# A planned attention-and-mixer kernel on one core: row sums, split loads, an uneven last chunk and small-tile products in one change

## The chip, the cores and the metric

One Trainium2 chip, one of its NeuronCores. TensorE (PE) does the matrix products, VectorE (DVE), ScalarE (ACT) and GpSimd (POOL) the rest, SyncE (SP) issues nearly all transfers. The metric is the device time of one execution in microseconds (us); less is better. Three timed runs of the kernel before gave 359.39, 359.53 and 359.98 us.

## The reference, cut to what matters

Linear attention over 8 batches of 8 heads, 576 tokens and 64 dimensions, then a mixer block on the 512 joined columns. All inputs and the output are float32.

```python
kv = einsum('bhsd,bhse->bhde', k, v)          # 64 x 64 for each head
out = einsum('bhsd,bhde->bhse', q, kv)
x = out / sqrt(mean(out * out, -1) + 1e-6) * g_norm      # heads joined: [8, 576, 512]
a1 = alpha1 * x + beta1
u = x + lam * einsum('ts,bsd->btd', w_tok, a1)           # w_tok: 576 x 576
a2 = alpha2 * u + beta2
result = u + lam * (maximum(a2 @ w_ch1, 0) @ w_ch2)      # 512 -> 2048 -> 512
```

The term `beta1` of `a1` goes through the token weight as (row sum of `w_tok`) times `beta1`. So the kernel carries one extra row beside the transposed token weight: the 576 row sums.

## The kernel before, in words

**Stages.** For each batch: the product k.v for 64 x 64 blocks (L691 for batch 0 and batches 2 to 7, L794 and L804 for batch 1), the product q.kv (L924 and L947 for batch 0 in float32; L1012, L454 and L1095 later), the norm, the token mixing (L1238 for batch 0, then L1161, L1213, L1192), the first channel layer (L1339, L1351, L1324 for even batches, L1366 for odd ones) with a relu on ACT, and the second channel layer (L1415; L1396 for the last 128 tokens). The 576 tokens of a batch are four chunks of 128 and a tail of 64; the tails of two batches are joined into a fifth chunk of the odd batch.

**The start.** Batch 0 needs everything at once: SP loads k, v and q of batch 0 by halves of four heads, then the token weight (L1516 and L1519, staged in the buffer `ht`), then batch 1 and the channel weights. q.kv of batch 0 (L915) multiplies 64-row by 128-column pieces of the transposed q by 64 columns of kv. The token weight is transposed by TensorE in five groups (L1556, `wt_groups`, L1546) and a tail group (L1570); ACT and DVE copy each to `wt` in bf16. Its row sums were made by TensorE: ten products of `wt` with a selecting matrix `sel` (L1592), whose result row is copied to row 64 of the fifth piece of `wt`. The product of that piece (the `rtt,wt` rows of L1238) needs the row.

**The order of the work** is made by a planner in the kernel's own text. Every operation is recorded with an engine, a cost, and what it reads and writes (L73). `plan` (L125) ranks operations by the time to the marked ones (`due`, L1656) and lays them out with `schedule` (L177), eight times over; a table of numbers then moves single operations (L1732). `schedule` books each load with a length (`dma_us`) and 1.75 us to completion (L348). It also books TensorE's instructions in blocks of 256 and lets no operation start whose block has not come by its table (L209). Until the first marked operation (the first channel layer of batch 0) is placed, TensorE is given a small product on zeros (L1728, called a filler here) wherever the plan has nothing ready for it. Fillers are real instructions: they take their time on the chip whether or not the wait exists there. `synchronize` (L370) then puts in the waits.

**The end.** The last 128 tokens of the last batch (`halves`, L1389) are done as two pieces of 256 output columns: 16 products, an addition on DVE (L1402) and a store (L1405) each.

## Time and profile before

| what | value |
|---|---|
| timed runs, median | 359.53 us |
| the profiled execution's own time | 358.89 us |
| its span, first to last instruction | 357.0 us |
| TensorE busy | 348.2 us (98%) |
| VectorE, ScalarE, GpSimd busy | 235.9, 157.1, 24.5 us |
| granted TensorE clock | 1.000 |

The profile is of one execution. A row of the chain of waits has a start, a length and what ran; a row of a timeline adds the shapes and, in brackets, idle time of the engine ahead of the row and what ended it. A group's row has the busy time, the mean of one instruction in ns, and the idle time before. Matrix products overlap in the array, so a single one's length (379 ns for 512 columns) is more than its share of the engine; the step from one start to the next is the price.

### The profile page before, as it was taken

How to read it: one execution, taken by the hardware profiler on the slowest of the kernel's cores; microseconds unless marked ns; L12 is line 12 of the kernel's file. 1: busy time of each engine (PE TensorE's matmuls, PEld its weight loads, DVE VectorE, ACT ScalarE, POOL GpSimd, SP SyncE). 2: the span in 40 equal slices, each digit the busy share in tenths (PEclk: the TensorE clock that was granted, in tenths of full speed). 3: DMA queues.
4: the chain of work that ended last, by engine and by line, in shares of the span. 5: the costliest groups of instructions: out<-in, count | busy, mean ns of one | idle time of the engine just before them, and what ended most of it. 6: DMA issues, size and time to landing. Idle time of an engine off the chain costs nothing.

```text
span 357.0 us, 7694 instructions
## 1 busy us (share of the span) xinstructions
PE 348.2 (98%) x3460; PEld 203.9 (57%) x3278; DVE 235.9 (66%) x359; ACT 157.1 (44%) x274; POOL 24.5 (7%) x31
## 2 busy tenths in 40 slices
PE   8999999999999999999999999999999999999996
PEld 6777554487645544467644554457644554457644
DVE  3577899778982489947884389957984378830021
ACT  3454981258810494028810386018830285007500
POOL 4153032700000000000000000000000000000000
PEclk9999999999999999999999999999999999999999
DMA  8999999789457830599257870395145010150022
GB/s 282 355 344 360 404 342 369 277 142 277 160 132 210 274 137 3 118 196 326 103 118 152 243 271 0 73 207 166 30 113 153 31 31 0 31 160 3 0 59 88
DMA packets 79896, 60.15 MB, mean 169 GB/s; under 512 B 53037, under 2 KB 63541, under 8 KB 79736
## 3 DMA queue, kind: packets, MB, share of 16 engines
q1 hardware_dynamic: 79840, 59.67, 56.5%
q8 instruction: 26, 0.43, 0.5%
q14 instruction: 6, 0.05, 0.0%
q10 hardware_dynamic: 24, 0.01, 0.0%
HBM read 38.82 MB, written 9.44 MB: 135 GB/s over the span
## 4 chain that ended last, share of the span: by engine, by line
PE 94%; DVE 2%; issue 1%; DMA 1%; ACT 0%; SPq 0%
PE ps L1415 31%; PE ps L1366 20%; PE ps L1324 14%; PE ps L1161 7%; PE ps L691 5%; PE ps L1012 2%; PE ps L454 2%; PE ps L1192 1%; PE ps L1238 1%; DMA vf<-in_v_dram 1%; PE ps L1273 1%; PE ps L924 1%; PE ps L1396 1%; PE ps L1213 1%; PE ps L1095 1%
## 5 line engine op out<-in xcount | busy, mean ns | idle before, releaser
L1415 PE MATMUL ps<-w,ht 128*128 128x512 bf16 x538 | 122.1, 379 | 2.1 <-issue 1.4
L1415 PEld LDWEIGHTS ps<-w,ht 128*128 128x128 bf16 x560 | 53.6, 98 | 63.7 <-issue 2.0
L1313 ACT ACTIVATE ht<-ps,hb 128x512 bf16<-128x512 f32 (+1 forms) x96 | 70.9, 739 | 43.2 <-PE ps L1366 31.8
L1366 PE MATMUL ps<-a2t,w 128*128 128x320 bf16 (+1 forms) x512 | 72.4, 299 | 0.0
L1366 PEld LDWEIGHTS ps<-a2t,w 128*128 128x128 bf16 x512 | 49.4, 98 | 20.2
L1324 PE MATMUL ps<-a2t,w 128*128 128x512 bf16 x231 | 53.3, 379 | 0.8 <-issue 0.5
L762 ACT ACTIVATE kvd<-ps 64x128 bf16<-64x128 f32 x24 | 6.5, 272 | 94.5 <-PE ps L691 94.3
L1425 DVE TENSOR_TENSOR xm<-ps,xm 128x512 f32<-128x512 f32 x31 | 20.7, 688 | 29.7 <-PE ps L1415 29.6
L1324 PEld LDWEIGHTS ps<-a2t,w 128*128 128x128 bf16 x240 | 22.6, 98 | 25.7
L1161 PE MATMUL ps<-rt,wt 128*128 128x512 bf16 x106 | 24.8, 379 | 0.3
L1034 DVE TENSOR_REDUCE small<-sq 128x16 f32<-128x1024 f32 x14 | 16.9, 1214 | 9.1 <-ACT sq L1032 9.0
L1314 ACT ACTIVATE ht<-ps 128x512 bf16<-128x512 f32 (+1 forms) x32 | 20.2, 655 | 3.0 <-PE ps L1324 1.8
L1174 DVE TENSOR_TENSOR xm<-ps,xm 128x1024 f32<-128x1024 f32 x14 | 17.1, 1222 | 5.1 <-PE ps L1213 4.0
L767 DVE TENSOR_TENSOR kvd<-ps,kvd 64x128 bf16<-64x128 f32 x24 | 6.9, 289 | 20.3 <-ACT kvd L762 19.9
L691 PEld LDWEIGHTS ps<-vf,kf 64*64 64x64 f32 x1008 | 16.0, 135 | 5.9 <-issue 4.8
L691 PE MATMUL ps<-vf,kf 64*64 64x64 f32 x1008 | 17.9, 221 | 0.5 <-DMA vf<-in_v_dram 0.5
L1161 PEld LDWEIGHTS ps<-rt,wt 128*128 128x128 bf16 x112 | 10.9, 98 | 12.9 <-issue 0.4
L646 DVE TENSOR_TENSOR qs<-qf,qs 128x1024 bf16<-128x1024 f32 x14 | 16.9, 1218 | 0.8 <-ACT qs L560 0.7
L1053 DVE TENSOR_TENSOR xm<-ps,small 128x1024 f32<-128x1024 f32 x14 | 17.1, 1224 | 0.4
L1425 DVE TENSOR_TENSOR xtl<-ps,xtl 128x512 f32<-128x512 f32 x4 | 2.8, 692 | 21.1 <-PE ps L1415 21.0
L1180 DVE TENSOR_TENSOR a2b<-xm,a_bc 128x512 bf16<-128x512 f32 x24 | 15.5, 688 | 0.4
L1012 PEld LDWEIGHTS ps<-kvd,qt 128*128 128x128 bf16 x224 | 14.1, 98 | 2.4
(148 smaller groups left out, 349.2 us busy)
## 6 DMA issues: line engine op xcount, KB each, us to landing
out_dram<-xm SPq DMA_DIRECT2D x31, 256.0 KB, 2.7
qf<-in_q_dram SPq DMA_DIRECT2D x7, 1024.0 KB, 7.7
kf<-in_k_dram SPq DMA_DIRECT2D x6, 1152.0 KB
vf<-in_v_dram SPq DMA_DIRECT2D x6, 1152.0 KB, 9.6
stg<-in_moe_w_ch_dram SPq DMA_DIRECT2D x3, 1024.0 KB, 13.7
kf<-in_moe_w_ch_dram SPq DMA_DIRECT2D x2, 1024.0 KB
kf<-in_k_dram SPq DMA_DIRECT2D x2, 576.0 KB, 4.7
vf<-in_v_dram SPq DMA_DIRECT2D x2, 576.0 KB, 6.2
```

Source lines behind the costliest of these rows:

```text
L646: lambda e, hi=hi, lo=lo, src=src: e.tensor_tensor(out=lo, in0=src, in1=hi, op=ALU.subtract), r=kin + kh, w=kl, port=True)
L691: m = e.matmul(t.ap(slice(64 * x, 64 * x + 64))[:, y, 0:64], nine(kf, b, a)[r, x, c, :], nine(vf, b, a)[r, x, c, :], start=(c == 0), stop= ...
L1012: e.matmul(o, w, kvd[:, h, 0, :], start=True, stop=False)
L1053: P.op("DVE", dve_us(64 * m), lambda e: e.tensor_tensor(out=x3, in0=split(raw()), in1=inv, op=ALU.mult), r=[t, ("sm", sms)], w=xk, pri=-200)
L1161: m = e.matmul(t.ap()[:, i, :], tok_w(sc, c), rsrc(b, sc), start=(sc == 0), stop=(sc == 4))
L1174: P.op("DVE", dve_us(512 * n), lambda e: e.tensor_tensor(out=x, in0=t.ap(rows) if n > 1 else t.flat(rows), in1=x, op=ALU.add), r=[t] + xk, ...
L1313: o = P.op("ACT", act_us(n) + 0.07 * (b > 1), lambda e: e.activation(dst, src(), ACT.Relu, bias=hb[:, fj:fj + 1]) if b > 1 else e.activati ...
L1314: dst, src(), ACT.Relu, bias=hb[:, fj:fj + 1]) if b > 1 else e.activation(
L1324: m = e.matmul(t.flat(), w, a2t[:, dj, 0:512], start=(dj == 0), stop=(dj == 3))
L1366: m = e.matmul(t.ap()[:, i, 0:n], w1[:, dj, 128 * fj:128 * fj + 128], a2t[:, dj, 320 * i:320 * i + n], start=(dj == 0), stop=(dj == 3))
L1415: m = e.matmul(t.flat(), ht[:, fj, 128 * c:128 * c + 128], w2[:, fj, :], start=(fj == 0), stop=(fj == 15))
L1425: P.op("DVE", dve_us(512), lambda e: e.tensor_tensor(out=x, in0=t.flat(), in1=x, op=ALU.add), r=[t] + keys, w=keys)
```

## The change

**Row sums from the loaded rows.** The selecting matrix and the ten products at L1592 go. Instead each of the five pieces of the loaded token weight (four of 128 rows, one of 64, each 576 columns wide) is summed along its columns by ACT or DVE into one column of a new tile `rs`, and five float32 products with the identity turn these columns into one row, which is copied to `wt`. **Two loads.** The token weight's first 512 rows come in two loads instead of one, and the transposes are grouped by load: six groups of four or two transposes instead of five groups of four. **q.kv in quarters.** For batch 0 each product of 128 columns becomes two of 64: twice the products, each in a quarter of the array. **The last chunk** is split into 384 and 128 columns. **The plan** gets other lengths for several transfers, a time to completion for each of the transposing transfers, more marked operations (all of the first layer of batch 1, the second layer of batch 1, the first operation of batch 2) and a new table of 42 moves.

```diff
-    def op(self, eng, cost, fn, r=(), w=(), pri=0.0, dma_us=None, port=False, ins=8):
+    def op(self, eng, cost, fn, r=(), w=(), pri=0.0, dma_us=None, port=False, ins=8, after=1.75):
...
-                        pick.end = dma_free + 1.75
+                        pick.end = dma_free + pick.after
...
-        sel = sb("sel", [128, 128], BF16)
+        rs = sb("rs", [128, 5], F32)
...
-                        w=[("qt", c, 0), ("qt", c, 1)], dma_us=2.0)
+                        w=[("qt", c, 0), ("qt", c, 1)], dma_us=1.3, after=0.9)
...
-                            for x in range(2):
-                                kr = slice(64 * x, 64 * x + 64)
-                                o = 256 * c + 64 * h
-                                mm = e.matmul(ts[x].flat()[:, o:o + 64], qt32[kr, 4 * a + h, c, :],
-                                              kv32[kr, a, (h + 2 * x) % 4, :], start=True,
-                                              stop=True, skip_group_check=True)
+                            for sh in range(2):
+                                for x in range(2):
+                                    kr = slice(64 * x, 64 * x + 64)
+                                    o = 256 * c + 64 * h
+                                    mm = e.matmul(
+                                        ts[x].flat(slice(64 * sh, 64 * sh + 64))[:, o:o + 64],
+                                        qt32[kr, 4 * a + h, c, 64 * sh:64 * sh + 64],
+                                        kv32[kr, a, (h + 2 * x) % 4, :], start=True, stop=True,
+                                        skip_group_check=True)
...
-                    r=[("a2b", c)], w=[("a2t", c)], pri=-200, dma_us=1.0)
+                    r=[("a2b", c)], w=[("a2t", c)], pri=-200, dma_us=0.8, after=1.0)
...
-                for i in range(2):
-                    t, cols = P.ptile(1), slice(256 * i, 256 * i + 256)
+                for lo, n in ((0, 384), (384, 128)):
+                    t, cols = P.ptile(1), slice(lo, lo + n)
...
-        P.op("SP", 0.6, lambda e: e.dma_start(
-            wst, moe_w_tok[0:512, :].rearrange("(p c) s -> p c s", c=4)),
-            w=["wst"], dma_us=3.3)
+        for i in range(2):
+            P.op("SP", 0.6, lambda e, i=i: e.dma_start(
+                wst[:, 2 * i:2 * i + 2, :],
+                moe_w_tok[0:512, :].rearrange("(p c) s -> p c s", c=4)[:, 2 * i:2 * i + 2]),
+                w=[("wst", i)], dma_us=1.6)
...
+            def total(i):
+                dst = rs[:, i:i + 1] if i < 4 else rs[0:64, 4:5]
+                src = wst[:, i, :] if i < 4 else wst2
+                junk = w1[:, i, 0:576] if i < 4 else w1[0:64, 0, 576:1152]
+                key = ("wst", i // 2) if i < 4 else "wst2"
...
+                    if e is nc.scalar:
+                        return e.activation(junk, src, ACT.Identity, accum_out=dst)
+                    return e.tensor_reduce(out=dst, in_=src, axis=AX.X, op=ALU.add)
...
-                    for sc in range(5):
-                        n = 128 if sc < 4 else 64
-                        m = e.matmul(t.flat()[:, 0:hi - lo], sel[0:n, :], wt[0:n, sc, lo:hi],
-                                     start=(sc == 0), stop=(sc == 4))
+                    for tc in range(5):
+                        n = 128 if tc < 4 else 64
+                        i = OFF[tc] if tc < 4 else 4
+                        m = e.matmul(t.flat()[:, 128 * tc:128 * tc + n],
+                                     rs[0:n, i:i + 1].to_broadcast([n, 128]), ident[0:n, 0:n],
+                                     start=True, stop=True, skip_group_check=True)
...
-            elif (b, ch, i) == (1, 0, 0):
-                due[o] = 36
+            elif (b, ch) == (1, 0) and i == int(i):
+                due[o] = 36 + 1.1 * i
+            elif (b, ch) == (1, 1):
+                due[o] = 56 + 0.87 * i
+            elif (b, ch, i) == (2, 0, 0):
+                due[o] = 78
```

How TensorE's instructions stand, at three places. The lines of the changed kernel are a few numbers further on: L1728 became L1772 (fillers), L924 L927, L947 L952, L691 L693, L1556 L1564, L1570 L1587, L1238 L1243, L1592 gave way to L1633, L794 L796. A float32 product that stands once here is two instructions in the trace.

First place, TensorE from the two small products that end the parameters (L1471, now L1476) to the transposes of the token weight. Before:

```order
L1728 MATMUL ps<-a2b 128x512 x2
L924 MATMUL ps<-kvd,qt 128x64 x16
L691 MATMUL ps<-vf,kf 64x64 x16
L947 MATMUL ps<-kvd,qt 64x64 x4
L1728 MATMUL ps<-a2b 128x512 x3
L691 MATMUL ps<-vf,kf 64x64 x20
L726 MATMUL ps<-ident,qf 128x128 x8
L1728 MATMUL ps<-a2b 128x512 x4
L741 MATMUL ps<-ident,qft 128x64 x2
L924 MATMUL ps<-kvd,qt 128x64 x16
L947 MATMUL ps<-kvd,qt 64x64 x4
L1728 MATMUL ps<-a2b 128x512
```

and of the change:

```order
L1772 MATMUL ps<-a2b 128x512 x3
L952 MATMUL ps<-kvd,qt 64x64 x4
L1772 MATMUL ps<-a2b 128x512
L927 MATMUL ps<-kvd,qt 64x64 x32
L1772 MATMUL ps<-a2b 128x512 x3
L693 MATMUL ps<-vf,kf 64x64 x36
L728 MATMUL ps<-ident,qf 128x128 x8
L743 MATMUL ps<-ident,qft 128x64 x2
L1772 MATMUL ps<-a2b 128x512 x3
L1564 MATMUL ps<-ident,ht 128x128 x8
L952 MATMUL ps<-kvd,qt 64x64 x4
L1564 MATMUL ps<-ident,ht 64x128 x2
```

The second k.v product is no longer cut in two; transposes of the token weight now stand ahead of the second half of q.kv (which follows these rows as 32 products of L927), and ten fillers have stayed ten.

Second place, TensorE around the token mixing of batch 0. Before:

```order
L1728 MATMUL ps<-a2b 128x512
L1238 MATMUL ps<-rt,wt 128x256 x12
L1592 MATMUL ps<-wt,sel 128x512 x5
L1592 MATMUL ps<-wt,sel 128x64 x5
L1238 MATMUL ps<-rt,wt 128x256 x4
L1728 MATMUL ps<-a2b 128x512 x2
L1238 MATMUL ps<-rtt,wt 128x256 x4
```

and of the change:

```order
L1772 MATMUL ps<-a2b 128x512 x7
L1243 MATMUL ps<-rt,wt 128x256 x16
L1633 MATMUL ps<-ident,rs 128x128 x4
L1633 MATMUL ps<-ident,rs 128x64
L1772 MATMUL ps<-a2b 128x512
L796 MATMUL ps<-vf,kf 64x64 x16
L1243 MATMUL ps<-rtt,wt 128x256 x4
```

Seven fillers stand where one stood, one where two stood, the ten sums are five products, and the first k.v product of batch 1 has moved up ahead of the mixing's last piece.

Third place, TensorE from the token mixing of batch 2 to its first channel layer. Before:

```order
L1161 MATMUL ps<-rt,wt 128x512 x16
L1213 MATMUL ps<-rtt,wt 128x512 x4
L1415 MATMUL ps<-w,ht 128x512 x60
L691 MATMUL ps<-vf,kf 64x64 x36
L1415 MATMUL ps<-w,ht 128x512 x8
L691 MATMUL ps<-vf,kf 64x64 x36
L1415 MATMUL ps<-w,ht 128x512 x4
L1324 MATMUL ps<-a2t,w 128x512 x8
```

and of the change, from the products of the second layer of batch 1 that now stand ahead of the mixing:

```order
L1420 MATMUL ps<-w,ht 128x512 x24
L1100 MATMUL ps<-kvd,qt 64x64 x16
L1420 MATMUL ps<-w,ht 128x512 x16
L1166 MATMUL ps<-rt,wt 128x512 x16
L1420 MATMUL ps<-w,ht 128x512 x4
L1218 MATMUL ps<-rtt,wt 128x512 x4
L1420 MATMUL ps<-w,ht 128x512 x36
L693 MATMUL ps<-vf,kf 64x64 x72
L1329 MATMUL ps<-a2t,w 128x512 x12
```

Of the second layer of batch 1, 72 products stood between the mixing of batch 2 and its first layer; now 36 do, and 40 of them stand between the second main piece of q.kv of batch 2 and the mixing, where 72 products of the first layer (L1366) and 8 of the second stood.

More of the change, by code (lines that the diff above doesn't have):

```diff
@@ L24 @@
     __slots__ = ("eng", "cost", "fn", "deps", "alloc", "tiles", "pri", "idx",
-                 "start", "end", "pos", "waits", "inc", "lat", "ring", "clock", "port", "follow", "ins")
+                 "start", "end", "pos", "waits", "inc", "lat", "after", "ring", "clock", "port", "follow", "ins")
     def __init__(self, eng, cost, fn, pri, idx):
@@ L1603, in run @@
+            yield row
         def run(gens):
```

102 lines of the change are left out of this document (61 added, 41 removed), and 9 rows, old and new, of the table start.

## The prediction

> **What bounds the kernel now.** I read the busy time by stretch first. The first row below is the start, up to the first channel layer of batch 0; the second runs from there to the last product; the third is the end. Columns: length, then busy time (and instructions) of PE, its weight loads, DVE, ACT, POOL, then granted clock, DMA share, GB/s.
>
> ```profile
> 5.99:34.05 28.06, 27.48 (x430) 22.14 (x436) 19.56 (x41) 13.50 (x33) 9.61 (x12) 1.00 1.05 353
> 34.05:353.70 319.65, 316.43 (x2986) 177.94 (x2798) 214.70 (x314) 142.07 (x240) 11.08 (x7) 1.00 0.53 152
> 353.70:357.00 3.30, 0.03 (x1) 0.00 (x0) 0.43 (x1) 0.00 (x0) 0.00 (x0) 1.00 0.12 41
> ```
>
> PE is busy for 316.43 of 319.65 us in the middle. Its list of waits says what the rest is:
>
> ```profile
> PE ps L1415 <- issue: 1.4, 9, 0.2
> PE ps L691 <- DMA vf<-in_v_dram: 0.5, 1, 0.5
> PE ps L1324 <- issue: 0.5, 3, 0.2
> ```
>
> Twelve gaps of about 0.16 us, each "issue", that is, for nothing another engine does. So the middle cannot become shorter by a better order; it can only become longer by new waits. What the change can win lies in the 28.06 us of the start and the 3.30 us of the end. For the start I use the chain of waits, whose steps are PE's own (start, length, what):
>
> ```profile
> 7.27 1.05 PE ps L1495 x2
> ...
> 10.52 1.93 PE ps L924 x32
> 12.45 0.62 PE ps L691 x32
> ...
> 13.47 0.59 PE ps L1728 x2
> 14.06 0.74 PE ps L691 x40
> ...
> 16.96 1.79 PE ps L924 x31
> 18.75 0.38 PE ps L947 x8
> ...
> 22.73 1.47 PE ps L1238 x12
> 24.20 1.54 PE ps L1592 x10
> 26.28 0.43 PE ps L1728 x2
> ...
> 33.50 0.39 PE ps L804 x16
> ```
>
> Even here PE never idles longer than 0.16 us, because the plan has put fillers (L1728) where it foresaw waits. The price of the start is therefore the sum of PE's instructions, fillers included.
>
> **The start, term by term.** All terms lie on PE, which sets the end.
>
> Sums removed: the ten products at L1592, -1.54.
>
> Row added: five float32 products, ten instructions, eight of 128 columns and two of 64, 1152 columns in all. The nearest row is L1495, float32 with 512 columns: two instructions, 1024 columns, 1.05 us. So 1152 / 1024 x 1.05 = +1.18. Were only one pass needed it would be 0.59; that is the lower bound.
>
> Quarters: now 1.93 + 0.06 + 1.79 = 3.78 us for 64 instructions, 59 ns each. The nearest row for the new shape is the k.v product of a later batch, same 64 x 64 pieces, same 64 columns, same cycling through four quarters:
>
> ```profile
> 114.93 1.21 PE ps L691 x72
> ```
>
> 16.8 ns each; 128 instructions cost 2.15. The upper bound is L804, also in quarters but short: 0.39 us for 16, 24.4 ns, so 3.12. I take the first, since the new runs are 64 long: -1.63 (bounds -1.63 and -0.66). The Trainium skill, "TensorEngine Tiling (Array Packing)", section "Instruction Overhead", says that each matmul has about 60 cycles of overhead, so that one should not tile a dimension that is already small; with the 2.4 GHz of the Trainium skill, "Trainium Kernel Development and Optimization", section "NeuronCore Architecture", that is an estimated 25 ns a piece, 3.2 us, and would leave of the start's sum below about nothing. L691's 16.8 speaks against it, L804's 24.4 for it.
>
> Fillers: after the first k.v product there were 13, now 18 (the order rows: ten stay ten, three become eight). Two cost 0.43, so five cost +1.08. The second k.v product in one piece, 1.21 for 0.62 + 0.74: -0.15.
>
> Sum of the start: -1.54 + 1.18 - 1.63 + 1.08 - 0.15 = -1.06. The first layer starts near 33.0 instead of 34.05.
>
> **What must hide.** The row sums go to DVE (three) and ACT (two). A DVE reduction of 512 columns is half of the first row here; the others are two loads, with their issue (start, length) and, from the list of transfers, KB and us to landing:
>
> ```profile
> 13.13 1.28 DVE L897 TENSOR_REDUCE small<-sq 128x8 f32<-128x512 f32 x2 [2.84 <-ACT sq L895]
> 6.74 0.59 SPq L1516 DMA_DIRECT2D ht<-in_moe_w_tok_dram x1
> ht<-in_moe_w_tok_dram SPq DMA_DIRECT2D x1, 1152.0 KB, 10.0
> 14.89 1.65 SPq L604 DMA_DIRECT2D vf<-in_v_dram  x1
> vf<-in_v_dram SPq DMA_DIRECT2D x1, 1024.0 KB, 8.9
> ```
>
> With 576 columns about 0.7 each, 2.1 us more on DVE between 15 and 20 us. Cover: the seven fillers (1.5 us) ahead of the mixing, which stood at 22.73 and comes to 22.73 - 1.63 - 0.15 + 6 x 0.216 = 22.25. By my count q.kv's second half ends near 19.6; two squares and two reductions, each step about 0.6, bring DVE to 21.6, and a copy of the token weight to 22.1. Without the fillers 1.4 us of that would show. The first reduction waits for the first load; queued behind it on DVE are a reciprocal and the second multiplication (L905) of the first half, which POOL and then the mixing wait for. The old load landed at 6.74 + 10.0 = 16.7; half of it, 576 KB at 353 GB/s, is 1.6 us, so the first part should land near 15.1, before DVE is there at 15.4. Were it to land at 16.7 instead, the multiplication would be 1.3 later, with POOL's step behind it still 2 us ahead of the mixing. Nothing shows.
>
> SP is held too: the loads of batch 1 wait for the first 16 products of the second k.v, which end near 13.9 instead of 13.07, since all of q.kv's first half now precedes them. Behind that wait stand all the loads of batch 1 and of the weights. The token weight's transfers run until past 16.7, so the engines do not dry out, and batch 1's v, issued at 14.89 with 8.9 to land, comes by 24.6 for PE's use near 25.7. I take 0; the bound is 0.8 if the whole train of loads moves.
>
> **The end.** The rows, and two of the transfer list (KB, us to landing):
>
> ```profile
> 36.15 0.89 PE ps L669 x16
> 350.23 3.51 PE ps L1396 x32
> 353.76 0.43 DVE xm L1402
> 17.54 0.58 DVE L967 TENSOR_TENSOR xtl<-ps,small 64x128 f32<-64x128 f32 x2
> out_dram<-xm SPq DMA_DIRECT2D x31, 256.0 KB, 2.7
> out_dram<-xm SPq DMA_DIRECT2D x2, 128.0 KB, 1.9
> ```
>
> PE: 384 columns by 512's share (0.43 / 2 x 0.75) are 16 x 0.162 = 2.60; 128 columns by L669 0.89; 3.49 for 3.51, nothing. The last addition is 0.29 (half of L967's row) for 0.43: -0.14. The last store has 64 KB for 128: between 0 and -0.4 (half of 2.7 - 1.9); I take -0.16, low because a store of 192 KB is now under way 0.7 us ahead of it. Together -0.3.
>
> **The middle.** The same work in another order; each gap I find can only be a loss. Two places have thin cover. One is the second quarter of w1, which by my count ACT finishes casting about when PE asks for it. The other is batch 2, worked out under the rivals, where my margins are 0.3 to 0.8 us. Durations that I know to 0.2 us do not settle such margins, so I take +0.3, bounds 0 and 2.3.
>
> **Sum**: -1.06 - 0.3 + 0.3 = -1.06. Against the profiled execution's own 358.89 (span 357.0 and 1.89 around it) that is 357.83. The median of the timed runs, 359.53, is 0.64 above that execution, so I forecast 358.5 for the median.
>
> **Rivals.** *Batch 2 loses its cover (slower).* These rows carry it: the end of q.kv and the last step before the mixing, the mixing's end, the add and the first products behind it, the transposes, the first layer, and what transposes take to land (q's, then those of a2).
>
> ```profile
> 86.15 0.19 PE L454 MATMUL ps<-kvd,qt 128*128 128x64 bf16 x1
> 93.25 1.23 DVE L1067 TENSOR_TENSOR rt<-sq,lam_bc 128x1024 bf16<-128x1024 f32 x1
> 101.27 0.60 PE L1213 MATMUL ps<-rtt,wt 64*128 64x512 bf16 x4
> 101.92 1.23 DVE L1174 TENSOR_TENSOR xm<-ps,xm 128x1024 f32<-128x1024 f32 x1 [0.86 <-PE ps L1213]
> 103.17 1.29 DVE L1180 TENSOR_TENSOR a2b<-xm,a_bc 128x512 bf16<-128x512 f32 x2
> 104.52 5.20 SPq L1303 DMA_TRANSPOSE a2t<-a2b  x4
> 119.98 1.24 PE L1324 MATMUL ps<-a2t,w 128*128 128x512 bf16 x5
> DMA to landing us min/median/max: 2.8/2.9/4.9
> DMA to landing us min/median/max: 2.3/2.4/3.6
> ```
>
> Before, the last of four transposes was issued at 104.52 + 3.9 = 108.4 and landed at 110.8; PE needed it at 119.98: 9 us to spare. In the change 36 products and the k.v products stand between, 36 x 0.216 + 2.42 = 10.2 us. The chain is two adds (2.45) and the first product of a2 (0.65), the last of four issues 3.9 later and 2.4 to land: 9.4. Spare 0.8. Four transposes of q follow on SP; the first two land at 9.4 + 3.1 = 12.5 for 12.8, the others at 15.0 for 15.5. Ahead of it, the chain from q.kv to the mixing took 94.48 - 86.15 = 8.3 us before and now has 40 x 0.216 + 0.37 = 9.0. If transposes land at the longest seen (a2t 3.6, qt 4.9) and DVE is 0.7 late, 0.4 + 1.5 + 0.4 = 2.3 us show: -1.36 + 2.3 = +0.9, 360.5. It is slower by my bound once the waits in the middle pass 2.1 us. For it: median landings are planned for where longer ones were before. Against: the plan counts the same queues. Chance 0.17.
>
> *Instructions come too late (no change).* Two rows of the profile's page, engines and the queue of the code:
>
> ```profile
> PE 348.2 (98%) x3460; PEld 203.9 (57%) x3278; DVE 235.9 (66%) x359; ACT 157.1 (44%) x274; POOL 24.5 (7%) x31
> q8 instruction: 26, 0.43, 0.5%
> ```
>
> PE's 6738 instructions in 26 packets are 259 each. From the first to the last half of q.kv PE took 322 in 8.2 us (25.6 ns each); now it would take 476 in 8.15 (17.1 ns). The trace has one stretch as dense (from 114.93 to 119.98, 156 products with their weight loads), but only 1.2 packets long. If the second packet is late at the old pace, 476 x 8.5 ns is 4.0 us at most; one packet late by a quarter of that, 1.0, gives -1.36 + 1.0, 359.2. Chance 0.09. The Trainium skill, "Runtime: NRT & Kernel Launch", section "Instruction fetch mechanics", has blocks of 256 fetched ahead and the cost mostly hidden; by that nothing would show here. The 26 packets agree with the size of the block; nothing here shows the fetch itself.
>
> *Small pieces are dear (no change).* Quarters at L804's 24.4 ns: +0.97, so 359.4. This is also what the Trainium skill's "TensorEngine Tiling (Array Packing)", section "Instruction Overhead", would give. For it: the 8 instructions of L947 took 0.38. Against: L691 has the same shape and length. Chance 0.07.
>
> *ACT and DVE set the start (no change).* The saved PE time turns into waits ahead of the mixing, +0.9, 359.4. For it: the plan has seven fillers there. Against: they already are in the sum. Chance 0.09. The Trainium skill, "TensorEngine Tiling (Array Packing)", section "PSUM Bottleneck", has this as a rule: tiling makes TensorE faster and not the copies out of PSUM.
>
> *More is won.* One pass for the row (-0.6) and no wait in the middle (-0.3): 357.6. Chance 0.08.
>
> **How the numbers follow.** The forecast has 0.50. About 0.2% (0.72 us) is what a measurement here can tell from no change. Faster is the forecast and "more is won", 0.58; within 0.2% the three rivals marked so, 0.25; slower 0.17. The range reaches from a little under "more is won", 357.3, to 360.6, just past batch 2's case; the forecast's own range is 357.8 to 358.8.
>
> **What would show it.** In the profile after: the first layer (L1344) starting at 33.0 +- 0.3; L927 in two runs of about 1.1 us; L1633 at 1.2; 18 fillers. A wait of PE on DVE or ACT at L1243 in place of its 0.05 would speak for the copies, "issue" gaps over 0.3 between 11 and 20 us for late instructions, waits at L1166, L1329 or L1017 between 95 and 130 us for batch 2. If the first layer starts at 33.0 and the time has not fallen, the middle has given it back. If L1344 starts later than 33.6, the sum of the start is wrong.

## The result, and where the profile says the time went

The changed kernel took 364.84 us (median; 363.91 to 365.19), the kernel before 359.61 in the same session: a ratio of 1.0145, 95% interval 1.0127 to 1.0163. It is 5.2 us slower; forecast was 358.5 and a gain. The profiled execution spans 363.4 us for 357.0, 6.4 more. All ratios here leave out executions over 1.5% above the fastest of their kernel: one of `before_shift` (371.20 us, mean clock 0.949) and two of `quarters_few` (363.84 and 364.30).

The stretches of the changed kernel, cut as those of before (start, middle, end; columns as in the prediction):

```profile
6.14:33.82 27.68, 27.28 (x502) 21.61 (x503) 17.28 (x37) 16.21 (x40) 11.27 (x14) 1.00 1.09 310
33.82:360.49 326.67, 322.54 (x3026) 177.55 (x2799) 215.96 (x324) 141.26 (x229) 13.20 (x8) 0.99 0.58 153
360.49:363.40 2.91, 0.00 (x0) 0.00 (x0) 0.29 (x1) 0.00 (x0) 0.00 (x0) 1.00 0.26 90
```

The middle grew by 7.0 us, and the end shrank by 0.4. Before the start can be compared, a reading of mine has to be mended. Two groups of PE in the kernel before, and the same two after (line, shape, count, busy time, mean ns, idle before):

```profile
L1415 PE MATMUL ps<-w,ht 128*128 128x512 bf16 x538 | 122.1, 379 | 2.1 <-issue 1.4
L1339 PE MATMUL ps<-a2t,w 128*128 128x512 bf16 x7 | 1.7, 379 | 0.2 <-issue 0.2
```

```profile
L1420 PE MATMUL ps<-w,ht 128*128 128x512 bf16 x560 | 125.5, 379 | 0.0
L1344 PE MATMUL ps<-a2t,w 128*128 128x512 bf16 x8 | 2.0, 380 | 0.0
```

Both programs have 560 and 8 of these products. In the profile of before 22 records and one are missing, and the "issue" gaps that I had read as 0.16 us of idle time stand where a record is missing (0.216 less a modelled overlap). So the first layer of before began one product earlier than I read, at 34.05 - 0.22 = 33.83, and that of the changed kernel at 33.82: the start won nothing, the middle lost 6.7, the end won 0.35 (3.26 to 2.91).

Where the middle lost it, PE's list of waits says (us in total, times, longest):

```profile
PE ps L1371 <- ACT ht L1318: 2.3, 1, 2.3
...
PE ps L1017 <- DMA qt<-qs: 0.9, 1, 0.9
PE ps L1017 <- ACT ht L1319: 0.4, 1, 0.4
PE ps L728 <- DMA qf<-in_q_dram: 0.4, 1, 0.4
PE ps L693 <- DMA vf<-in_v_dram: 0.4, 1, 0.4
PE ps L1329 <- DVE w L563: 0.3, 1, 0.3
PE ps L671 <- DVE qs L648: 0.2, 1, 0.2
```

I compared the start of each run of products with the sum of the prices ahead of it, in both kernels. By that the changed kernel falls behind at four places, 6.7 us in all: 0.8 us at 39 to 41 us (w1's cast and q's low half), 0.7 at 90, 1.0 at 125 (q's transposes), 4.2 at 172 to 179. The last, on ACT:

```profile
169.87 0.30 ACT L1042 ACTIVATE small<-small,eps 128x16 f32<-128x16 f32 x1
173.49 0.63 ACT L562 ACTIVATE qs<-qft 64x512 bf16<-64x512 f32 x1 [3.33 <-DMA qft<-in_q_dram]
174.13 0.79 ACT L1318 ACTIVATE ht<-ps,hb 128x640 bf16<-128x640 f32 x1
```

The cast of the last 64 rows of batch 5's q stands ahead of a relu of batch 3's first layer and waits 3.33 us for its load; the relu behind it frees the PSUM bank that PE needs. And the 2.3 us in which PE stood still were not all. The stretches around it (PE's busy time and count first, granted clock in the third column from the end):

```profile
172.00:175.00 3.00, 0.67 (x6) 0.26 (x5) 2.97 (x4) 1.50 (x3) 0.00 (x0) 1.00 1.03 330
175.00:176.00 1.00, 1.00 (x7) 0.69 (x8) 0.83 (x1) 1.00 (x2) 0.00 (x0) 0.83 1.05 389
176.00:177.00 1.00, 1.00 (x5) 0.55 (x4) 0.00 (x0) 0.84 (x2) 0.00 (x0) 0.50 1.05 392
177.00:178.00 1.00, 1.00 (x5) 0.60 (x4) 0.18 (x1) 0.79 (x2) 0.00 (x0) 0.50 0.89 329
178.00:179.00 1.00, 1.00 (x6) 0.58 (x4) 1.00 (x2) 0.15 (x1) 0.00 (x0) 0.50 0.29 106
179.00:180.00 1.00, 1.00 (x9) 0.69 (x8) 0.37 (x1) 0.65 (x1) 0.00 (x0) 0.97 0.04 14
```

For 3.4 us the clock was 0.50, five products a microsecond for nine: 1.7 us more.

All these waits end on a load, or on a cast, a relu or a transpose behind one. The row that shows why stands in the third part of the profile's page: packets, MB, and their time as a share of 16 engines' span. Before and after:

```profile
q1 hardware_dynamic: 79840, 59.67, 56.5%
```

```profile
q1 hardware_dynamic: 79984, 59.67, 60.8%
```

The same 59.67 MB took 56.5% of 357.0 = 201.7 us, then 60.8% of 363.4 = 220.9: 9.5% longer. The issues of batch 1's first load and of two later ones on SP, before and after, show what that does:

```profile
13.14 0.37 SPq L604 DMA_DIRECT2D kf<-in_k_dram  x1
...
23.56 1.81 SPq L1630 DMA_DIRECT2D w<-in_moe_w_ch_dram  x1
...
28.93 1.35 SPq L1454 DMA_DIRECT2D lam_bc<-in_moe_lam_dram  x1
```

```profile
14.58 0.38 SPq L606 DMA_DIRECT2D kf<-in_k_dram  x1
...
26.38 1.50 SPq L1670 DMA_DIRECT2D w<-in_moe_w_ch_dram  x1
...
31.85 1.73 SPq L1459 DMA_DIRECT2D lam_bc<-in_moe_lam_dram  x1
```

1.4 us late at the first, 2.8 and 2.9 at the others. The first experiments are about the waits; what slows the transfers comes after them.

### The profile page after: what moved, and what is told of

Same layout as the page of the kernel before. It is cut to its first block, busy times and chain, and to the rows that moved or that the text cites. A ratio compares the mean times of both kernels' runs of the same rounds, so it can differ in the third digit from the quotient of the medians.

```text
span 363.4 us, 7882 instructions
## 1 busy us (share of the span) xinstructions
PE 354.4 (98%) x3570; PEld 203.4 (56%) x3346; DVE 235.3 (65%) x367; ACT 159.0 (44%) x270; POOL 27.9 (8%) x32
## 3 DMA queue, kind: packets, MB, share of 16 engines
q1 hardware_dynamic: 79984, 59.67, 60.8%
## 4 chain that ended last, share of the span: by engine, by line
PE 81%; DMA 11%; SPq 3%; DVE 3%; ACT 1%; issue 0%
PE ps L1420 33%; PE ps L1371 15%; PE ps L1329 13%; PE ps L1166 7%; DMA qf<-in_q_dram 5%; DMA qft<-in_q_dram 4%; PE ps L693 4%; PE ps L1017 2%; PE ps L456 2%; PE ps L1197 1%; SPq L611 1%; DMA qt<-qs 1%; PE ps L1401 1%; PE ps L1218 1%; PE ps L1278 1%; PE ps L1100 1%
## 5 line engine op out<-in xcount | busy, mean ns | idle before, releaser
L1420 PE MATMUL ps<-w,ht 128*128 128x512 bf16 x560 | 125.5, 379 | 0.0
L1371 PE MATMUL ps<-a2t,w 128*128 128x320 bf16 (+1 forms) x512 | 73.6, 304 | 2.3 <-ACT ht L1318 2.3
L1371 PEld LDWEIGHTS ps<-a2t,w 128*128 128x128 bf16 x512 | 50.1, 99 | 23.7 <-ACT ht L1318 2.7
L1329 PE MATMUL ps<-a2t,w 128*128 128x512 bf16 x240 | 54.6, 379 | 0.3 <-DVE w L563 0.3
L1166 PE MATMUL ps<-rt,wt 128*128 128x512 bf16 x112 | 25.8, 379 | 0.0
L693 PEld LDWEIGHTS ps<-vf,kf 64*64 64x64 f32 x1008 | 15.9, 135 | 5.4 <-issue 3.8
L693 PE MATMUL ps<-vf,kf 64*64 64x64 f32 x1008 | 17.7, 221 | 0.4 <-DMA vf<-in_v_dram 0.4
L1017 PE MATMUL ps<-kvd,qt 128*128 128x64 bf16 x224 | 14.8, 193 | 1.3 <-DMA qt<-qs 0.9
L1430 DVE TENSOR_TENSOR xtl<-ps,xtl 128x512 f32<-128x512 f32 x4 | 2.8, 689 | 20.2 <-PE ps L1420 20.1
```

Of the source, the lines that this page charges most:

```text
L693: m = e.matmul(t.ap(slice(64 * x, 64 * x + 64))[:, y, 0:64], nine(kf, b, a)[r, x, c, :], nine(vf, b, a)[r, x, c, :], start=(c == 0), stop= ...
L1017: e.matmul(o, w, kvd[:, h, 0, :], start=True, stop=False)
L1166: m = e.matmul(t.ap()[:, i, :], tok_w(sc, c), rsrc(b, sc), start=(sc == 0), stop=(sc == 4))
L1329: m = e.matmul(t.flat(), w, a2t[:, dj, 0:512], start=(dj == 0), stop=(dj == 3))
L1371: m = e.matmul(t.ap()[:, i, 0:n], w1[:, dj, 128 * fj:128 * fj + 128], a2t[:, dj, 320 * i:320 * i + n], start=(dj == 0), stop=(dj == 3))
L1420: m = e.matmul(t.flat(), ht[:, fj, 128 * c:128 * c + 128], w2[:, fj, :], start=(fj == 0), stop=(fj == 15))
```

## The experiments

Each ratio is against the kernel before in the same session (359.06 to 359.52 us there), since sessions differ by 0.1%. The changed kernel's is 1.0145.

**The casts.** The plan is told that two loads land 4 us later, so that it puts the casts behind the relus.

```diff
 def load_tail(...):
-                dma_us=0.75)
+                dma_us=0.75, after=5.75 if b == 5 else 1.75)    # late_cast5
+                dma_us=0.75, after=5.75 if b in (3, 5) else 1.75)    # late_cast
```

> The changed kernel with one step moved: ACT's cast of the last 64 rows of batch 5's q stands behind two relus of batch 3's first layer instead of ahead of them (the plan is told that this load lands 4 us later); no other engine's order changes. Theory A (the wait and its aftermath): the 2.33 us in which PE waits for the relu at 172.6 us goes, and with it the 3.4 us at half clock that follow it (1.7 to 1.9 us); 364.8 - 4.2 = 360.6, give or take 0.4. Rival B (the load itself is late, the cast only shows it): the wait moves on to the transposes and the q.kv products of batch 5, and the time stays at 363 to 365. Rival C (the half clock has another cause): only the wait goes, 362.5, and the profile still shows about 3.4 us at a granted clock of 0.5.

Measured: 362.39, 1.0091 (1.0071 to 1.0112). In its profile the wait and the half clock are gone and the span is 359.4, 4.0 less, as theory A said; by the ratios it won 1.9. The changed kernel's other three executions had a mean clock of 1.000 where the profiled one had 0.995, so they had no such slow stretch; their waits were not profiled. A's place is right, and its price is that of one execution.

> As the run before, and the same for the cast of batch 3's q, behind which the relu of batch 1's first layer is late by 0.4 us at 90 us (0.67 us in all beside PE's price of the products there). Theory A: 360.6 - 0.6 = 360.0. Rival B: no change from the run before, since batch 3's transposes then come later and the wait for them at 125 us, 0.9 now, grows by as much.

Measured: 361.37, 1.0070 (1.0053 to 1.0086). The wait at 90 us is gone, as theory A said; the 0.8 us less are not clear of noise, since the intervals of the two runs overlap. The two casts together are worth 2.7 us of the 5.2, at the changed kernel's addresses.

`late_cover` puts two groups of batch 2's first layer ahead of the q.kv product that waits 1.0 us. Expected was 1.0 us less if the transposes alone are late (theory A), or no change if the wait moves (rival B):

```diff
-        P.plan(due, 8, {..., 452: -3.1, 482: 25.9})
+        P.plan(due, 8, {..., 452: -3.1, 482: 25.9, 521: 25, 536: 26})    # on late_cast
```

> The changed kernel with the two casts late, and with two more groups of batch 2's first layer (L1329, 0.87 us each) ahead of batch 2's first q.kv product, which waits 1.0 us for q's transposes at 125 us. Theory A (the transposes are late, PE has other work): the wait goes, 361.4 - 1.0 = 360.4. Rival B (the wait moves: the products put ahead need PSUM banks that ACT's relus free, or the mixing of batch 3 comes too late by the same 1.0): 361.4.

Measured: 362.45, 1.0096 (1.0081 to 1.0110): rival B, and worse. The wait at 125 us is gone, and a new one of 1.3 stands at L1371 for the transposes of a2. Moving covers about does not pay for late transfers.

**The start.** `quarters` and `quarters_end` put one and two parts of the change into the kernel before, whose order stays as it was.

```diff
+                            for sh in range(2):      # quarters: L924's 128 x 64 as two 64 x 64
...
-                for i in range(2):                   # quarters_end: and the last chunk
+                for lo, n in ((0, 384), (384, 128)):
```

> The kernel before with one edit: batch 0's q.kv in quarters, 128 products for 64; the order on every engine stays as it was. Theory A (PE's own price decides, copies are hidden behind the fillers): each half of q.kv takes 1.1 us for 1.9, the first channel layer starts 1.5 us earlier than the 33.83 of before, and the time is 359.6 - 1.5 = 358.1. Rival B (the copies of ACT and DVE, or the loads, set the start): new waits of PE between 12 and 30 us eat the gain, first layer at 33.3 to 33.8, 359.1 to 359.6. Rival C (what is won in the start is given back by waits further on, for loads that don't come earlier): first layer at 32.3, waits of PE between 34 and 80 us, 359.1 to 359.6.

> As the run before, and the last chunk as 384 and 128 columns. The end from PE's last product to the end of the span goes from 3.26 to 2.91 us, as in the changed kernel; 0.35 less than the run before: 357.75 by theory A, 358.8 to 359.3 by B and C. Rival for the end: the last store is not what ends the run, 0 for it.

Measured: 358.87, 0.9989 (0.9981 to 0.9998), and 357.97, 0.9966 (0.9954 to 0.9978). Each half of q.kv by itself took about 1.1 us as priced, but the first layer began at 33.93 and 33.75: theory A falls, and B holds in its effect. Of what PE waited for, 0.9 us were v's loads (0.5 before), which is B's, and 0.5, named "issue", is new. The second half of q.kv in `quarters` (time, us, what), and all of PE's work up to that gap (products and weight loads in brackets):

```profile
17.00 1.03 PE L925 MATMUL ps<-kvd,qt 64*64 64x64 f32 x53
18.56 0.39 PE L925 MATMUL ps<-kvd,qt 64*64 64x64 f32 x10 [0.53 <-issue]
```

```profile
0.00:18.55 18.55, 15.86 (x348) 12.11 (x348) 8.43 (x22) 7.26 (x19) 5.79 (x15) 1.00 0.91 315
```

The gap stands after 348 products and 348 loads. To see whether that is chance, I left out fillers (`after_nofill` in the changed kernel, `quarters_end_nofill`, and `quarters_end_some`, only those behind the 352nd product) or merged the early ones (`quarters_few`):

```diff
-    lambda e, cols=cols: self.warm[1](e, self.warm[3], cols),
+    lambda e, cols=cols, t=t: None if t > 9.0 else      # _some: t > 19.0
+    self.warm[1](e, self.warm[3], cols),
...
+    n = len(self.warm[3].ops) if t < 5.9 else 0          # quarters_few
+    lambda e, n=n: None if n % 4 else self.warm[1](e, self.warm[3], 512),
```

> The changed kernel without the 18 fillers that stand behind the first k.v product (4.3 us of PE's start); every other instruction in the same order. Theory A (the fillers cover the delivery of PE's instructions and the copies): PE waits about as long in their places, gaps named issue in front of the rows that contain the 224th and the 352nd product of PE's stream and a wait on ACT or DVE at L1243; the first layer starts between 32.5 and 33.8 (33.82 with them), the time is 363.5 to 364.8. Rival B (the fillers are waste, PE's own price sets the start): nothing takes their place, first layer at 29.5, 360.5. Rival C (idle time lets the clock fall): stretches at a granted clock of 0.5 behind the gaps, slower than 364.8.

> Quarters alone in the kernel before, and the first 43 warm-up products of 128 columns merged four by four into products of 512 columns: the same PE time before the first k.v product, 64 instructions fewer (products and weight loads), same order. Quarters alone has gaps of 0.5 to 1.0 us at the 224th and the 352nd product of PE's stream, which are 256 instructions apart. Theory A (instructions come in blocks of 256; a block is there only some 5.4 to 6.1 us after PE has begun on the block two ahead of it): with fewer instructions early PE enters the second block later, at about 10 us instead of 7, so the third is there at 16 instead of 13, where it is needed at 13.5 to 15: a gap of 1 to 2.5 us between 14 and 17 us, first layer 0.3 to 1.5 later than with quarters alone (33.9), 359.2 to 360.4. Rival B (the gaps come from the number of instructions as such, so fewer of them is sooner): both gaps shrink, first layer at 33.0, 358.0. Rival C (they were loads): the first gap, beside the load of v, stays as it is, the second too; 358.9.

> Quarters and the 384 + 128 columns in the kernel before, and the 13 fillers behind the first k.v product left out. Theory A (delivery of instructions sets the point at the 352nd product, 18.5 us): nine fillers ahead of it are 18 instructions, so 0.4 is won there, and up to 0.9 from the four fillers behind it if nothing else waits there: first layer at 32.5 to 33.4 (33.75 with them), 356.8 to 357.7. Rival B (all are waste): 30.9, 355.2. Rival C (ACT and DVE, or loads, take their place): 33.7, 358.0, with waits of PE on them at the mixing (L1241).

> Quarters and the 384 + 128 columns in the kernel before, and only the four fillers behind the 352nd product left out (0.9 us); without any filler the mixing started at 22.1 us with no wait on ACT or DVE, and in some executions the clock fell behind the 0.9 and 1.2 us for which PE then stood still. Theory A (instructions are the floor up to the 352nd product, fillers keep the clock there; behind it nothing waits): first layer near 32.9, 358.0 - 0.9 = 357.1, no execution with a lowered clock. Rival B (the four cover waits on copies or loads): 358.0, first layer at 33.75, with a wait of PE on ACT, DVE or a load in front of L1241 or L794.

`quarters_end_nofill`, the rows behind its two gaps and the counts up to them:

```profile
13.18 0.28 PE L692 MATMUL ps<-vf,kf 64*64 64x64 f32 x4 [0.90 <-issue]
...
18.26 0.27 PE L926 MATMUL ps<-kvd,qt 64*64 64x64 f32 x1 [1.19 <-issue]
```

```profile
0.00:13.17 13.17, 11.03 (x221) 9.06 (x221) 4.83 (x12) 5.08 (x11) 3.79 (x12) 1.00 0.88 308
0.00:18.25 18.25, 14.66 (x348) 12.15 (x348) 8.52 (x22) 7.28 (x19) 6.10 (x15) 1.00 0.91 312
```

221 and 348 again, 127 products with 127 loads apart: 254 instructions beside what the count leaves out. The gaps of `quarters_end` (0.99) and `after_nofill` (0.92) also stand after 221, in the middle of a run of products, those of `quarters_few` (0.26 and 0.28) after 219 to 221 and 343 to 348, though it issues 64 instructions fewer before them. By this PE's instructions come in blocks of about 256, whatever stands in them (no trace shows the fetch itself), and where PE waited at the two boundaries it passed them at 13.1 to 13.4 and 18.3 to 18.6 us (in `quarters_few` at 14.6 and 20.8). Quarters add 32 products and as many loads to each half. They use up the instructions sooner than these come.

The four results: `after_nofill` 363.72, 1.0129 (1.0112 to 1.0147), theory A in kind (its first layer at 34.3 is later than the range given), with these waits in the fillers' place:

```profile
PE ps L1244 <- DVE wt L564: 1.1, 1, 1.1
...
PE ps L1565 <- DMA ht<-in_moe_w_tok_dram: 1.0, 2, 0.7
PE ps L694 <- issue: 0.9, 1, 0.9
...
PE ps L729 <- DMA qf<-in_q_dram: 0.6, 2, 0.3
...
PE ps L797 <- DMA vf<-in_v_dram: 0.3, 1, 0.3
```

Of these, 3.6 us stand behind the first k.v product (0.3 of L729's lie ahead of it, as in the changed kernel). The 18 fillers took 4.3 us, and without them the first layer comes no earlier: they are waits under another name. `quarters_few` 361.28, 1.0045 (1.0017 to 1.0072): the places are theory A's, the size isn't (0.26 for 1 to 2.5), and its executions spread from 358.5 to 364.3, the cause of which stays open. `quarters_end_nofill` 357.77, 0.9968 (0.9948 to 0.9988): first layer at 32.8 (theory A), but three of twelve executions, those with a mean clock of 0.990 to 0.995, took 359.3 to 360.8, the others 356.9 to 358.1. None of the three was profiled, so where their clock fell is not shown. `quarters_end_some` 357.66, 0.9955 (0.9942 to 0.9969): between A and B, its profiled first layer at 33.3 behind a wait of 1.25 us for v's load. It has the lowest ratio here, but its interval overlaps those of `quarters_end` and `quarters_end_nofill`.

**Plan or parts?** Without the table of priority shifts the planner's own order can be compared with old and new parts under the old prices.

```diff
-        P.plan(due, 8, {171: -35.6, ...})
+        P.plan(due, 8, {})      # before_notable; parts_notable: the four parts of the change as well
```

> The kernel before without its table of priority shifts, so that the planner's own order stands. The planner itself gives it 2.0 us more than with the table; if its prices hold on the chip, 359.1 + 2.0 = 361.1. It serves as the base for the next run.

> All parts of the change (row sums from the loaded rows, token weight in two loads, q.kv in quarters, last chunk as 384 + 128) under the plan of the run before: its prices, its due times, no table. Theory A (the new plan lost the time, the parts themselves are worth a little: 0.35 at the end, 0.3 to 0.6 in the start): 0.3 to 1.0 less than the run before. Rival B (the parts lost it, whatever the plan: quarters and row sums make the start's copies and instructions late): 3 to 5 us more than the run before.

Measured: 360.90, 1.0039 (1.0024 to 1.0054), and 363.88, 1.0118 (1.0099 to 1.0138). My theory A, that the new plan lost the time, falls: the parts cost 3 us under the old plan too. Their first layer starts at 35.6 for 34.5, with PE waiting 0.7 us for batch 1's v.

**Why are the loads late?** One load for two (a load of a single row that nothing reads stands in the second's place), and an earlier release of batch 1's loads, each with every order kept:

```diff
-        for i in range(2):                                        # late_one, on late_cast;
-            P.op("SP", 0.6, ... wst[:, 2 * i:2 * i + 2, :], ...)  # parts_notable_one, on parts_notable
+        P.op("SP", 0.6, lambda e: e.dma_start(wst, moe_w_tok[0:512, :]...), w=[("wst", 0)], ...)
+        P.op("SP", 0.6, lambda e: e.dma_start(hst[64:65, 2304:2880], moe_w_tok[512:513, :]), ...)
...
-            parts = ((range(4), ["gate"]), ...                    # late_gate, on late_cast
+            parts = ((range(4), ["gate0"]), ...
...
-                         w=ts)
+                         w=ts + (["gate"] if (a, j) == (0, 1) else []))
```

> The changed kernel with the two casts late (361.4), and the 512 rows of the token weight in one load again; in the second load's place stands one of a single row that nothing reads, so that every engine's order is the same. Theory A (the two loads make the transfers slower: with them 365, 364 and 310 GB/s between 8 and 14 us for 410, 401 and 416 before, and every later load comes 1.4 to 3.3 us later): about 400 GB/s there again, the first layer 0.3 to 0.5 earlier, and the 0.8 us of waits on w1's cast and on q's low half at 39 to 41 us gone: 360.3. Rival B (the transfers are slow for another reason, such as the later release of batch 1's loads): 310 to 365 GB/s as before, 361.4.

> All parts of the change under the plan of the kernel before without its table (363.9; first layer 35.6), with the token weight in one load, as in the run before. Theory A: the load of v for batch 1, 0.7 late at L796, and the waits behind it shrink; first layer at 34.8, 362.0 to 362.9. Rival B (the parts cost their 3 us in other ways: fillers and copies in the start, their order in the middle): 363.9, first layer at 35.6.

> The changed kernel with the two casts late (361.4), and batch 1's loads released by the end of the first half of q.kv instead of the first sixteen products of the second k.v: every order the same, the release some 1.3 us earlier (13.2 for 14.5). Theory A (what is late in the start's loads is their release): kf's load issued at 13.2, the later ones 1.3 earlier too, the waits at 39 to 41 us (0.8) gone, 360.6. Rival B (the transfers ahead of them are still under way, so an earlier issue only queues): issue at 13.2, landings as before, 361.4.

Measured: 362.38, 1.0108 (1.0064 to 1.0152); 365.17, 1.0165 (1.0136 to 1.0195); 361.19, 1.0060 (1.0044 to 1.0077). Rival B three times; the two with one load come out slower than their bases rather than equal (1.0108 for 1.0070, within the interval; 1.0165 for 1.0118, beyond it), with PE waiting 1.2 and 1.8 us for the token weight. With one load the transfers stay slow (`late_one`):

```profile
q1 hardware_dynamic: 79842, 59.67, 61.3%
```

61.3% of 360.5 is 221.0 us. With the early release kf's load is issued at 13.07 for 14.50, and the load of w at 26.85 for 26.73: it only queues. But this row sorts all the kernels run so far into two kinds: 200 to 206 us in all with the old row sums, 214 to 225 in all with the new. What the kinds differ in is the memory: the tensor `sel`, 256 bytes of a partition, gave way to `rs`, 20 bytes, which take 32. Every tensor allocated behind them moved down by 224 bytes: k, v, q and the staging of the weights from multiples of 256 bytes to 32 past them. The traces hold no addresses: the move follows from the tensors' sizes, and that the old places were multiples of 256 is shown by no run.

```diff
-        rs = sb("rs", [128, 5], F32)
+        rs = sb("rs", [128, 64], F32)      # after_pad, parts_notable_pad; late_pad: on late_cast
...
         sel = sb("sel", [128, 128], BF16)
+        sb("shift", [128, 16], BF16)       # before_shift: 32 bytes that nothing uses
```

> The changed kernel with the row sums' tensor 64 columns wide instead of 5, of which 5 are used: it then takes 256 bytes of a partition, as the removed tensor sel did, and every tensor behind it (k, v, q, the staging of the weights) stands again at an address that is a multiple of 256 bytes (the weight tile ht at 128 past one) instead of 32 bytes past it. Same instructions, same order, same loads. Theory A (the shifted addresses make the transfers slower): the packets of the load queue take about 202 us of the 16 engines again, as in every profile with sel (200 to 206), for 214 to 224 in every one without; 400 GB/s between 8 and 14 us; the loads of q land in time, so the waits behind the casts (2.7 us in the medians), most of the 0.8 at 39 us and 0.4 at the first q transposes go: 359.5 to 361. Rival B (the transfers are slow for something else in the parts, the order or the row sums): 215 to 224 us, 364.4. The Trainium skill, DMA: Bandwidth & Descriptors, section How a descriptor splits into AXI transactions, says that a piece that does not start on a 256-byte boundary takes one transaction more; for 1024-byte pieces that would be five for four.

> The kernel before with an unused tensor of 32 bytes a partition behind sel, so that every later tensor stands 32 bytes past its old address, as in the change; nothing else. Theory A: the packets take about 220 us instead of 202, loads land later, PE gets new waits on loads or on casts behind them; slower by 1 to 4 us: 360 to 363. Rival B: 202 us, 359.1, no change.

> All parts of the change under the plan of the kernel before without its table (363.9), with the row sums' tensor 256 bytes wide as in the first run here. Theory A: v of batch 1 lands in time at L796, first layer at 34.8 or earlier instead of 35.6, and fewer waits behind it; 361.0 to 362.5, against 360.9 for the old parts under the same plan. Rival B: 363.9.

Measured, `after_pad`: 360.11, 1.0018 (1.0004 to 1.0032), 4.6 us less than the changed kernel. Its packets took 55.2% of 358.3 = 197.8 us, and of the waits these two are left in the middle:

```profile
q1 hardware_dynamic: 79984, 59.67, 55.2%
```

```profile
PE ps L1371 <- ACT ht L1318: 1.2, 1, 1.2
...
PE ps L1017 <- DMA qt<-qs: 0.5, 1, 0.5
```

`before_shift`: 361.20, 1.0043 (1.0028 to 1.0058), 1.5 us slower by an unused tensor, with 61.5% of 360.1 = 221.5 us:

```profile
q1 hardware_dynamic: 79840, 59.67, 61.5%
```

The same loads go slower, from 409 GB/s to 339 (last column) between 8 and 14 us, before and in `before_shift`:

```profile
8.00:14.00 6.00, 5.68 (x90) 4.39 (x91) 1.78 (x5) 3.31 (x9) 0.00 (x0) 1.00 1.07 409
```

```profile
8.00:14.00 6.00, 5.68 (x89) 4.39 (x90) 1.44 (x4) 3.37 (x9) 0.00 (x0) 1.00 1.08 339
```

The changed kernel had 346 there, `after_pad` 384. q's transposes landed after 3.4 us (median) in `before_shift` and the changed kernel, after 2.9 before and in `after_pad`. The engines' own work did not slow down: DVE and ACT were busy for 235.7 and 157.4 us in `before_shift`, 235.9 and 157.1 before.

`parts_notable_pad`: 360.39, 1.0042 (1.0018 to 1.0065), 200.8 us, first layer at 34.2. Under the old plan the new parts now cost what the old ones do (1.0039). Theory A in all three (the last came out below its range); it is shown both ways, by undoing the shift alone and by making it alone.

> The changed kernel with both repairs: the row sums' tensor 256 bytes wide, so that the addresses are those of before, and the casts of the last 64 rows of q of batches 3 and 5 behind the relus. With the addresses alone it took 360.1, its first layer started 0.5 earlier than before, and its profile still shows 1.2 us of PE's wait for a relu behind the cast of batch 5 (1.6 in all) and 0.5 on q's transposes. Theory A (that cast is what is left): 360.1 - 1.6 = 358.5, faster than the kernel before (359.2). Rival B (with the loads on time the wait only moves to the next step of that chain): 360.1.

Measured: 359.13, 0.9996 (0.9987 to 1.0005). Between the two: 0.8 of the 1.6 expected, just clear of noise. Its profile spans 357.1, and of the middle's waits only that on q's transposes is left:

```profile
PE ps L1017 <- DMA qt<-qs: 0.5, 1, 0.5
```

So by the ratios 4.6 us of the loss were the addresses, which made the casts, w1 and the transposes late; 0.8 more goes with two casts placed without slack (the 2.7 that the casts gave by themselves overlap with the 4.6); and what remains of the change is no difference that can be measured. `quarters_end` is 0.3% faster than that with two of its parts and the old plan. Whether the row sums, the two loads or the new plan cost that 1.1 us was not tried.

## Why the prediction was wrong, step by step

**The failed step** is the sum's "+0.3 for the middle, bounds 0 and 2.3". It measured 6.7 in the profiled execution. I bounded each wait with transfers that land as they did before, "the longest seen" included, and priced instructions and issues only; the exchange of `sel` for `rs` was not in my list of what the change removes and adds. It moved nearly every on-chip tensor, and with them the pace of the transfers. With the addresses repaired the middle, from the first layer to the last product, is 322.0 us in `after_pad` and, with the casts late too, 320.7 in `late_pad`, for 319.9 before: +2.1 and +0.8, both inside the bounds.

**The second failed step** is the start's -1.06, which measured 0. Quarters took 1.09 us a half where I had 1.08: 17.0 ns a piece, so L691's 16.8 was the right row, not L804's 24.4. With it the estimate from the Trainium skill, "TensorEngine Tiling (Array Packing)", section "Instruction Overhead" (25 ns a piece), does not hold here. The row took 1.35 for 1.18, and there are 18 fillers. Yet the first layer came at 33.82, which by my own test means that the sum of the start is wrong. From the last product of the parameters (L1471, now L1476) to the first layer PE took 24.0 us before and 23.4 in the changed kernel, in `after_pad` and in `late_pad` alike: 0.6 was won of the 1.06. The row is 0.17 of what is missing; for the rest the cause stays open. In the changed kernel that 0.6 was lost again ahead of it, where the first k.v product came 0.15 later and PE waited 0.4 for q's first load. With the addresses repaired the first layer came at 33.4 and 33.5, 0.3 to 0.5 earlier than before. And `after_nofill` shows that fillers cannot simply be left out to win more: they stand for waits on instructions, copies and loads.

**"SP is held too ... I take 0; the bound is 0.8."** For the release itself 0 holds: `late_gate` released the loads 1.4 us earlier and no difference shows (1.0060 for 1.0070, intervals overlapping). But the loads came 1.4 us late at the first and 2.9 at a later one, because the transfers ahead of them were slower, which was not in the sum.

**"The first part should land near 15.1."** DVE's first reduction waited for it until 16.62, and PE until 16.7 in `after_nofill`; in the changed kernel three fillers at 16.3 covered it for PE. This is the later landing that the prediction had allowed for.

**"Instructions come too late" (rival, 0.09).** It named the mechanism, and its price of 1.0 is what `quarters_end` showed (0.99). In the changed kernel itself no "issue" gap over 0.3 shows between 11 and 20 us: without its fillers there is one of 0.92 (`after_nofill`).

**Batch 2 (rival, 0.17).** Right in kind and too small: 1.0 at q's transposes, 0.7 at 90 us, and not foreseen the 4.2 at batch 3. Of the wait on q's transposes (0.9 us) 0.5 is left with the addresses repaired, so part of it came from what the rival did not have. I looked for thin cover only where the order had changed most. w1's second quarter, named as "cast about when PE asks", did show (0.3), and went with the addresses.

**The end, -0.3.** -0.35, the last addition 0.29 as worked out.

**What bounds the kernel.** The middle was saturated, more than I said, since the twelve gaps were missing records and the 0.5 us on v in the same list stands at 5.99 us, where the start begins; that it could only lose was right.

## What to carry to other kernels

When a change adds or drops an on-chip tensor, look at the addresses of everything allocated behind it, and compare the packets' time for the same bytes, one row of the page, before explaining any wait. Fillers in a planned order are waits with a name: price what they cover, not their length. An engine's queue must not hold a step that waits for a load ahead of one on which the critical engine depends, unless the load's slack is larger than its spread.

## What was not expected of the hardware

On-chip tensors moved by 32 bytes (from multiples of 256 bytes to 32 past them, if the places are as counted above) made 59.67 MB take 221.5 us of packet time for 201.7, 9.8% longer (`before_shift`, nothing else changed). Most of it falls on small pieces: counted from the packets of the two traces, one of 256 bytes took 24.1 ns for 20.2, one of 1024 bytes 57.1 for 52.2, one of 2048 bytes 96.9 for 95.6. The 256-byte pieces make 12.1 of the 19.8 us, and by their number nine in ten of them belong to the transposing transfers. The Trainium skill, "DMA: Bandwidth & Descriptors", section "How a descriptor splits into AXI transactions", has such a rule, put for reads: a descriptor that does not start on a 256-byte boundary begins with a transaction from the boundary below it. By that it is, as an estimate, five transactions for four at 1024 bytes. The traces agree in the direction, with 9% at that size; only these two offsets were run.

PE's gaps "issue" stood after 221 and 348 products with as many weight loads in kernels of different orders, and the boundaries were 5.1 and 6.2 us apart in time in the two kernels where PE waited at both. The Trainium skill, "Runtime: NRT & Kernel Launch", section "Instruction fetch mechanics", has the block of 256, which agrees; that its fetch is mostly hidden does not hold in this start, where single gaps were 0.3 to 1.2 us.

After 2.3 us of standing still PE had 3.4 us at a granted clock of 0.50. The Trainium skill, "TensorE: Matmul & The Clock Gate", section "What's actually happening", gives such a window of about 3.4 us for each way. The length of the slow stretch agrees; but the fall came after 2.3 us of idling, and in `after_nofill` a wait of the same length at 90 us was followed by no fall, so a wait of this length cost 1.7 us more in one trace and nothing in another.
